# Moving the last 64 rows of a weight onto four DMA engines in a decode kernel: gated attention and MLP on one core

## The chip, the cores and the metric

The kernel runs on one core of a Trainium2 chip. The core has a matrix engine (TensorE; its matmuls are "PE" in the profile and its weight loads "PEld"), a vector engine (DVE), a scalar engine (ACT), a general engine (POOL), a sequencer that here only issues transfers (SP), and 16 DMA engines that carry data from the chip's memory (HBM) into the on-chip memory of 128 partitions (SBUF). The metric is the device time of one execution in microseconds.

## The reference

One decode step for a batch of 8 with a model width of 448. Attention: 16 query heads on 8 key/value heads, each 256 wide, over the last 1024 positions of the cache. Beside it a small MLP (448 to 1792 to 448). A sigmoid gate mixes the two. All tensors are bf16.

```
g = sigmoid((x * gate_w).sum(-1))
q = x @ wq                                   # 448 x 4096
p = softmax(q k^T * 256**-0.5)               # k, v: last 1024 rows of the caches
a = (p v) @ wo                               # 4096 x 448
b = gelu(layernorm(x) @ w1 + b1) @ w2 + b2
out = g * a + (1 - g) * b
```

The K and V that are read make 64 MB, wq and wo 3.5 MB each, w1 and w2 1.5 MB each.

## The kernel before

Everything is loaded once. SP issues nearly all transfers, in one written order: w1 (`w1_sb`, L159; its last 64 rows `w1_t`, L162), w2 (L164), three pieces of wq of 128 rows (`wq_sb`, L167), the last 64 rows of wq (`wq_t`, L168), and then a list of units: 32 K tiles and 32 V tiles of 1 MB (`load`, L148; one tile holds two batches of one head), and eight pieces of wo (`wo_sb`, L187), one behind every fourth K tile and the eighth at the very end. The last V tile comes in two halves. `issue_to` (L182) issues units as long as one of the 12 buffers for K and V is free; its first call, `issue_to(NKV)`, stands at L200, before the small constants are built. Each transfer that SP issues also waits until the transfer eight places earlier has landed, since eight completion counters are used in turn. x, b1, b2 and later gate_w are issued by ACT (L156 to L158, `gate_load`).

The small constants (an identity, ones, masks, zeroed pads) are written by DVE and POOL at L203 to L230. Then x and its normalised form y are turned into columns: `halves` spreads the last 64 entries of a row over even and odd places of two rows of 128, `transposed` turns five pieces with TensorE and copies the result to `xT` and `yT`. The MLP follows (`mlp_up` L311, `mlp_down` L347), then q: for each of 32 blocks of 128 columns of wq, the block is the stationary side and `xT` (8 columns) the moving side, so q comes out with its head dimension on the partitions. 96 matmuls take `wq_sb`, 32 take `wq_t` (L377), which holds each of the 64 rows as two half rows on two partitions. Two scaled copies (L389) write `qT`.

The main loop has 64 steps. A step turns half a K tile with 16 transposes (`transposes`, L407; copies L412), makes the scores of the step before (`scores`, L433), and eleven steps behind them the product with V (`pv`, L508). After four V tiles, `o_scale` (L519) and `o_proj` (L533) multiply a head's output by its piece of wo, into one PSUM bank that all heads share. At the end `o_proj(7)` runs 8 matmuls, DVE applies the gate (L577), and SP and ACT each send half of the result (L581).

Of the kernel before, what the change touches and what calls it, by code (L numbers as in the profile page):

```python
# [16 lines left out]
def kernel(  # L17
# [38 lines left out]
    HH = HD // 2  # L56
    assert Sq == 1 and Dh % P == 0 and W % P == 0 and F % P == 0
    FH = F // 2
    NH = NF // 2
    assert TL * 2 == P and NC * R <= 2 * P and NB % TB == 0 and 3 * 32 <= P and R <= 32 and NF % 2 == 0  # L60
    qscale = float(Dh) ** -0.5
    NU = NBU * Hkv
    NSTEP = NU * TB
# [2 lines left out]
    NKV = 12  # L66
# [4 lines left out]
    CP = 32  # L71
# [37 lines left out]
    wq_t = big.tile([P, HH], BF16, name="wq_t")  # L109
    w1_sb = big.tile([P, DC, F], BF16, name="w1_sb")  # L110
    wo_sb = [big.tile([P, NKH, D], BF16, name=f"wo_sb{g}") for g in range(Hkv)]
# [3 lines left out]
    gw_sb = consts.tile([NB, D], BF16, name="gw_sb")  # L115
# [11 lines left out]
    xT = consts.tile([P, DC + 2, NB], BF16, name="xT")  # L127
    yT = consts.tile([P, DC + 2, NB], BF16, name="yT")
    x_e = consts.tile([NB, 2, P], BF16, name="x_e")
# [11 lines left out]
    def load(kind, n):  # L141
        t = kvpool.tile([P, NC, Dh], BF16, tag="kv", name="kv")
        src = A_k_cache if kind == "K" else A_v_cache
        g, u = divmod(n, NBU)
        parts = TB if (kind, n) == ("V", NU - 1) else 1
        w = NC // parts
        for q in range(parts):
            nc.sync.dma_start(  # L148
                t[:, q * w : (q + 1) * w, :].rearrange("p c d -> p (c d)"),
                src[u * TB : (u + 1) * TB, g, kv0:Sk, :].rearrange(  # L150
                    "t (r c) d -> r t c d", c=NC
                )[:, :, q * w : (q + 1) * w, :].rearrange("r t c d -> r t (c d)"),
            )
        KV[kind, n] = t
# [27 lines left out]
    def issue_to(k):  # L182
        while pos[0] < len(units):
            kind, n = units[pos[0]]
            if kind == "W":
                r0 = n * NKH * P
                nc.sync.dma_start(  # L187
                    wo_sb[n][:].rearrange("p (i j) n -> p i (j n)", i=rep),
                    A_wo[r0 : r0 + NKH * P, :].rearrange(
                        "(i p j) n -> p i (j n)", i=rep, j=NJ  # L190
                    ),
                )
# [39 lines left out]
    prod = consts.tile([NB, D], F32, name="prod")  # L232
# [7 lines left out]
    y_sb = consts.tile([NB, D], BF16, name="y_sb")  # L240
# [27 lines left out]
    def transposed(dst, t, t_e):  # L268
        v = t[:, 0:DM].rearrange("b (p c) -> b c p", c=DC)
        parts = [v[:, c, :] for c in range(DC)] + [t_e[:, h, :] for h in range(2)]  # L270
        tp = ps_kt.tile([P, W], BF16, tag="ktp", name="tp")
        for c, part in enumerate(parts):
            nc.tensor.transpose(
                tp[:, c * NB : (c + 1) * NB], part, ident[0:NB, 0:NB]
            )
        nc.vector.tensor_copy(
            dst[:], tp[:, 0 : len(parts) * NB].rearrange("p (c b) -> p c b", b=NB)
        )

    halves(y_e, y_sb)  # L280
    transposed(yT, y_sb, y_e)
    halves(x_e, x_sb)
    transposed(xT, x_sb, x_e)


    def gate_load():
        src = gate_w.rearrange("(o d) -> o d", o=1)
        nc.scalar.dma_start(gw_sb[:], src.to_broadcast([NB, D]))

    def gate():  # L290
        nc.vector.tensor_tensor(prod[:], x_sb[:], gw_sb[:], op=ALU.mult)
# [13 lines left out]
        nc.vector.tensor_copy(gg4[:], A_bank[0:PT, DN : DN + 2])  # L305
        nc.vector.tensor_scalar_mul(bvec[:], bsum[:], gg4[:, 1:2])
# [58 lines left out]
    mlp_down()  # L365


    q_ps = ps_g.tile([P, 512], F32, tag="grp", name="q_ps")
    NQ = Hq * NJ
    for c in range(DC + 1):  # L370
        for k in range(NQ):
            if c < DC:
                w, xs = wq_sb[:, c, k * P : (k + 1) * P], xT[:, c, :]
            else:
                h, kk = divmod(k, NQ // 2)
                w, xs = wq_t[:, kk * P : (kk + 1) * P], xT[:, DC + h, :]
            nc.tensor.matmul(  # L377
                q_ps[:, k * NB : (k + 1) * NB],
                lhsT=w,
                rhs=xs,  # L380
                start=(c == 0 and k == 0),
                stop=(c == DC),
                skip_group_check=True,
            )
    q_v = q_ps[:, 0 : Hq * NJ * NB].rearrange(
        "p (g i j b) -> p i j g b", i=rep, j=NJ, b=NB
    )
# [158 lines left out]
    for n in range(LAST):  # L546
# [5 lines left out]
        g, r = divmod(n, SPG)  # L552
# [7 lines left out]
        m = n - SPG - LAG  # L560
# [51 lines left out]
```

## Time and profile before

| what | value |
|---|---|
| median of 3 runs | 196.95 us (196.83 to 197.05) |
| the profiled execution, its own time | 196.92 us |
| its span, first to last instruction | 195.2 us |
| busy: PE, PEld, DVE | 164.2, 153.6, 113.1 us |
| busy: ACT, POOL | 6.4, 2.8 us |
| moved | 78.14 MB, mean 400 GB/s |
| last 64 rows of wq | 1 transfer of 512 KB, 14.5 us from issue to landing |
| last piece of wo | 1 transfer of 448 KB, issued at 174.03 us, landed at 191.33 us |

The profile is one execution. It gives busy time by engine, the waits, the chain of work that ended last, and a record of each DMA packet with its queue, size, start and duration, though not the number of the DMA engine that carried it. Queue q1 holds what SP issues, q10 what ACT issues, q8 and q14 instructions that the chip fetches for its own engines. A packet is one run of bytes: a wq or K tile gives packets of 8 KB, `wq_t` of 4 KB, a wo piece of 1792 B. On each engine, a transfer ends with a packet of 4 B, which counts the completion.

### The profile page before, as it was taken

The numbers are of one execution on the slowest core, as the hardware profiler recorded it, in microseconds if no ns is written. First come the engines' busy times: TensorE is split into PE (matmuls) and PEld (weight loads), VectorE is DVE, ScalarE is ACT, GpSimd is POOL, SyncE is SP. The second block draws the span as 40 slices with busy tenths as digits, with TensorE's granted clock in tenths as the row PEclk, the third lists the DMA queues.
The fourth block names the chain that finished last, engine by engine and source line by source line (L and its number), as shares of the span: only waits on it lengthen the run. The fifth ranks groups of instructions, "written<-read, shape, count | busy, mean of one in ns | idle before, by whom it ended". The sixth has DMA issues, their size and how long they took to land.

```text
span 195.2 us, 7355 instructions
## 1 busy us (share of the span) xinstructions
PE 164.2 (84%) x3417; PEld 153.6 (79%) x3417; DVE 113.1 (58%) x255; ACT 6.4 (3%) x13; POOL 2.8 (1%) x16
## 2 busy tenths in 40 slices
PE   2677799988899796958999898988898989989752
PEld 1565799988899796957999797978897989989541
DVE  3122189996477653764559674964586646766401
ACT  5000000000000000010000000000000000000000
POOL 5000000000000000000000000000000000000000
PEclk9999889997569855585569996995599655699555
DMA  6999999999999999999999999999999999999940
GB/s 215 412 426 425 425 413 426 426 423 420 421 426 422 417 425 426 425 417 431 423 423 419 422 425 428 418 421 418 425 430 417 421 425 430 426 420 425 394 176 5
DMA packets 12769, 78.14 MB, mean 400 GB/s; under 512 B 1330, under 2 KB 3523, under 8 KB 4164
## 3 DMA queue, kind: packets, MB, share of 16 engines
q1 hardware_dynamic: 12688, 77.67, 95.4%
q8 instruction: 26, 0.43, 0.8%
q10 hardware_dynamic: 52, 0.02, 0.0%
q14 instruction: 3, 0.02, 0.0%
HBM read 77.68 MB, written 0.01 MB: 398 GB/s over the span
## 4 chain that ended last, share of the span: by engine, by line
DMA 91%; PE 6%; SPq 1%; issue 0%; DVE 0%
DMA kv<-in_A_k_cache_dram 47%; DMA kv<-in_A_v_cache_dram 19%; DMA wo_sb<-in_A_wo_dram 18%; DMA wq_sb<-in_A_wq_dram 7%; PE ktp L407 4%; PE grp L433 1%; PE A_bank L533 0%; PE grp L508 0%; SPq L167 0%; PE grp L422 0%; SPq L164 0%; DVE res L577 0%; SPq L159 0%; SPq L162 0%; SPq L148 0%
## 5 line engine op out<-in xcount | busy, mean ns | idle before, releaser
L412 DVE COPY kt<-ktp 128x1024 bf16<-128x1024 bf16 x128 | 84.4, 687 | 44.4 <-PE ktp L407 43.9
L407 PE MATMUL ktp<-ident,kv 128*128 128x128 bf16 x1024 | 89.0, 257 | 7.9 <-DMA kv<-in_A_k_cache_dram 6.7
L407 PEld LDWEIGHTS <-kv 128*128 128x128 bf16 x1024 | 78.0, 118 | 10.9 <-DMA kv<-in_A_k_cache_dram 7.9
L508 PE MATMUL grp<-e,kv 128*128 128x4 bf16 x1024 | 35.6, 166 | 2.6 <-DMA kv<-in_A_v_cache_dram 2.5
L508 PEld LDWEIGHTS <-kv 128*128 128x128 bf16 x1024 | 32.6, 101 | 5.6 <-DMA kv<-in_A_v_cache_dram 2.8
L433 PE MATMUL grp<-qT,kt 128*128 128x4 bf16 x1024 | 36.6, 166 | 0.3 <-DVE kt L412 0.2
L433 PEld LDWEIGHTS <-kt 128*128 128x128 bf16 x1024 | 34.6, 100 | 1.8 <-issue 0.6
L482 ACT ACTIVATE e<-grp 128x256 bf16<-128x256 f32 x8 | 3.1, 383 | 161.8 <-PE grp L475 161.8
L491 PE MATMUL A_bank<-zs,onesf 128*128 128x16 f32 x16 | 3.6, 299 | 4.5 <-DVE zs L487 4.5
L491 PEld LDWEIGHTS A_bank<-zs,onesf 128*128 128x128 f32 x16 | 2.8, 218 | 5.1 <-DVE zs L487 5.1
L533 PE MATMUL A_bank<-wo_sb,ot 128*8 128x224 bf16 x64 | 5.5, 305 | 0.8 <-DMA wo_sb<-in_A_wo_dram 0.5
L321 PE MATMUL h_ps<-yT,w_sb 128*128 128x8 bf16 x42 | 4.2, 195 | 1.2 <-DMA w_sb<-in_B_w_dram 1.2
L495 DVE RECIPROCAL rz<-A_bank 128x16 f32<-128x16 f32 x8 | 2.1, 258 | 5.4 <-PE A_bank L491 5.4
L519 DVE TENSOR_TENSOR ot<-grp,rz 128x32 bf16<-128x32 f32 x8 | 1.5, 186 | 6.4 <-PE grp L508 6.4
L487 DVE TENSOR_REDUCE zs<-e 128x16 f32<-128x256 bf16 x8 | 4.8, 602 | 0.0
L353 PE MATMUL b_ps<-w_sb,hT 128*8 128x224 bf16 x28 | 2.8, 388 | 2.4 <-DVE b_ps L349 2.4
L338 DVE COPY z<-h_ps 128x112 f32<-128x112 f32 x1 | 0.3, 275 | 7.7 <-PE h_ps L329 7.7
L321 PEld LDWEIGHTS <-w_sb 128*128 128x128 bf16 x42 | 3.6, 152 | 1.3 <-DMA w_sb<-in_B_w_dram 1.3
L475 PE MATMUL grp<-diag,onesb 128*128 128x256 bf16 x8 | 2.5, 308 | 2.2 <-DVE diag L469 1.9
L353 PEld LDWEIGHTS <-hT 128*8 128x8 bf16 x28 | 1.8, 121 | 3.0 <-DVE hT L344 2.2
L446 DVE TENSOR_REDUCE pm<-grp 128x16 f32<-128x256 f32 x8 | 3.3, 415 | 0.6 <-PE grp L433 0.6
L533 PEld LDWEIGHTS <-ot 128*8 128x8 bf16 x64 | 2.6, 93 | 1.3 <-issue 0.4
(82 smaller groups left out, 53.6 us busy)
## 6 DMA issues: line engine op xcount, KB each, us to landing
kv<-in_A_k_cache_dram SPq DMA_DIRECT2D x32, 1024.0 KB, 18.3
kv<-in_A_v_cache_dram SPq DMA_DIRECT2D x31, 1024.0 KB, 18.3
wo_sb<-in_A_wo_dram SPq DMA_DIRECT2D x8, 448.0 KB, 18.3
wq_sb<-in_A_wq_dram SPq DMA_DIRECT2D x3, 1024.0 KB, 12.1
w_sb<-in_B_w_dram SPq DMA_DIRECT2D x1, 1568.0 KB
w_sb<-in_B_w_dram SPq DMA_DIRECT2D x1, 1344.0 KB, 5.9
kv<-in_A_v_cache_dram SPq DMA_DIRECT2D x2, 512.0 KB, 19.8
wq_t<-in_A_wq_dram SPq DMA_DIRECT2D x1, 512.0 KB, 14.5
```

Source lines behind the costliest of these rows:

```text
L321: nc.tensor.matmul(o, lhsT=cols(w1_sb[:, c, h * FH : (h + 1) * FH]), rhs=yT[:, c, :], start=(c == 0), stop=False,)
L353: nc.tensor.matmul(b_ps[CP * j : CP * j + NB, 0:DN], lhsT=M["hT"][:, k * NB : (k + 1) * NB] if k < NF else onesb[0:1, 0:NB], rhs=w2_sb[:, ...
L407: nc.tensor.transpose(ktp[:, c * P : (c + 1) * P], K[:, h * HC + c, j * P : (j + 1) * P], ident[:],)
L412: nc.vector.tensor_copy(kt[:, j, :], ktp[:])
L433: nc.tensor.matmul(G[g][:, s : s + RU], lhsT=kt[:, j, c * P : (c + 1) * P], rhs=qT[:, j, g, bu * TB : (bu + 1) * TB, :].rearrange("p t i - ...
L446: nc.vector.reduce_max(pm[:], G[g][:, S0 : S0 + NC * R].rearrange("p (c r) -> p r c", r=R), axis=AXIS.X,)
L475: nc.tensor.matmul(G[g][:, S0 : S0 + NC * R].rearrange("p (c r) -> p c r", c=NC), lhsT=onesb[:], rhs=diag[g % 2][:].unsqueeze(1).to_broadc ...
L482: nc.scalar.activation(e[:], G[g][:, S0 : S0 + NC * R], ACT.Exp)
L487: nc.vector.reduce_sum(zs[:], E[g][:].rearrange("p (c r) -> p r c", r=R), axis=AXIS.X)
L491: nc.tensor.matmul(zc, lhsT=onesf[:], rhs=zs[:], start=False, stop=True, skip_group_check=True)
L508: nc.tensor.matmul(G[g][:, o : o + RU], lhsT=V[:, cc, :].rearrange("p (q j) -> p j q", j=NJ)[:, j, :], rhs=E[g][:, cc * R + bu * RU : cc * ...
L533: nc.tensor.matmul(A_bank[CP * j : CP * j + NB, 0:DN], lhsT=ot[:].rearrange("p j (b i) -> p j i b", i=rep)[:, h, i, :], rhs=wo_sb[g][:, k, ...
```

## The change

The last 64 rows of wq are stored and loaded in another way, and several things follow from it.

1. `wq_t` is no tile of its own any more. It is a view of the first 48 partitions of a new tile `wo_hi`, which later receives the wo pieces of heads 3 to 7. A partition holds two neighbouring rows of wq, a run of 16 KB; partitions 0 to 15 and 32 to 47 are used. Two transfers bring 16 partitions each, with a source written as 4 by 4 by 8192 elements. POOL first writes zeros over the 48 partitions. These transfers, and with them `issue_to(NKV)`, stand behind the small constants in the program.
2. q is computed with x as the stationary side (`xT` padded to 32 columns) and wq as the moving side, 512 columns at a time. Four matmuls write four strips of 32 partitions of one PSUM tile, for two tiles and five pieces of rows: 40 matmuls in place of 128. Then DVE and ACT each scale one tile into `q_r`, 8 transposes turn it, and four copies write `qT`.
3. `pairs` replaces `halves` for x, `transposed` makes two copies instead of one, and `xT` is zeroed by POOL.
4. The last piece of wo comes in two transfers of 224 KB.
5. `gw_sb` becomes a view of `w1_sb`.

```
-    nc.sync.dma_start(wq_t[:], A_wq[DM:D, :].rearrange("r (h n) -> (r h) n", h=2))
...
+    TQ, TH, TP = 2, 16, 48
+    NHI = 5
+    wo_sb = [big.tile([P, NKH, D], BF16, name=f"wo_sb{g}") for g in range(Hkv - NHI)]
+    wo_hi = big.tile([P, NHI * NKH * D], BF16, name="wo_hi")
+    wq_t = wo_hi[0:TP, 0 : TQ * HD].rearrange("p (q n) -> p q n", q=TQ)
...
+    gw_sb = w1_sb[0:NB, 0, 0:D]
...
-                nc.sync.dma_start(
-                    wo_sb[n][:].rearrange("p (i j) n -> p i (j n)", i=rep),
...
+                dst = wo_sb[n][:, :, :].rearrange("p (i j) n -> p i (j n)", i=rep)
...
+                if n < Hkv - 1:
+                    nc.sync.dma_start(dst, src)
+                else:
+                    for i in range(rep):
+                        nc.sync.dma_start(dst[:, i, :], src[:, i, :])
...
-    issue_to(NKV)
...
+    nc.gpsimd.memset(xT[:], 0.0)
...
+    nc.gpsimd.memset(wq_t, 0.0)
+    for h in range(2):
+        nc.sync.dma_start(
+            wq_t[32 * h : 32 * h + TH].rearrange("p q n -> p (q n)"),
+            A_wq[DM + TL // 2 * h : DM + TL // 2 * (h + 1), :].rearrange(
+                "(r i q) n -> i r (q n)", i=4, q=TQ
+            ),
+        )
+    issue_to(NKV)
...
+    def pairs(dst, src):
+        for h in range(2):
+            nc.vector.tensor_copy(
+                dst[:, :, 32 * h : 32 * h + TH].rearrange("b q (i r) -> b q i r", i=4),
+                src[:, DM + TL // 2 * h : DM + TL // 2 * (h + 1)].rearrange(
+                    "b (r i q) -> b q i r", i=4, q=TQ
+                ),
+            )
...
-    for c in range(DC + 1):
-        for k in range(NQ):
...
-            nc.tensor.matmul(
-                q_ps[:, k * NB : (k + 1) * NB],
-                lhsT=w,
-                rhs=xs,
...
+    for c, (w, xs) in enumerate(wq_c):
+        for t in range(NT):
+            for k in range(NS):
+                n0 = QW * (NS * t + k)
+                nc.tensor.matmul(
+                    q_ps[t][CP * k : CP * (k + 1), :],
+                    lhsT=xs,
+                    rhs=w[:, n0 : n0 + QW],
...
+                    tile_position=(0, CP * k),
...
-    for i in range(rep):
-        nc.vector.tensor_scalar_mul(qT[:, :, :, :, i], q_v[:, i], qscale)
+    nc.vector.tensor_scalar_mul(q_r[:, 0:QW], q_ps[0][:], qscale)
+    nc.scalar.activation(q_r[:, QW : 2 * QW], q_ps[1][:], ACT.Copy, scale=qscale)
+    q_tp = ps_kt.tile([P, W], BF16, tag="ktp", name="q_tp")
+    for t in range(NT):
+        for k in range(rep * NJ):
+            o = (t * rep * NJ + k) * P
+            nc.tensor.transpose(q_tp[:, o : o + P], q_r[:, o : o + P], ident[:])
...
+    for t in range(NT):
+        for i in range(rep):
+            nc.vector.tensor_copy(
+                qT[:, :, NS * t : NS * (t + 1), :, i], q_v[:, t, i, :, :, 0:NB]
+            )
```

More of the change, by code (lines that the diff above doesn't have):

```diff
@@ L55 @@
     TL = D - DM
-    HH = HD // 2
+    TQ, TH, TP = 2, 16, 48
     assert Sq == 1 and Dh % P == 0 and W % P == 0 and F % P == 0
@@ L59 @@
     NH = NF // 2
-    assert TL * 2 == P and NC * R <= 2 * P and NB % TB == 0 and 3 * 32 <= P and R <= 32 and NF % 2 == 0
+    assert TL * 2 == P and TL == 2 * TH * TQ and NC * R <= 2 * P and NB % TB == 0 and 3 * 32 <= P and R <= 32 and NF % 2 == 0
     qscale = float(Dh) ** -0.5
@@ L108 @@
     wq_sb = big.tile([P, DC, HD], BF16, name="wq_sb")
-    wq_t = big.tile([P, HH], BF16, name="wq_t")
     w1_sb = big.tile([P, DC, F], BF16, name="w1_sb")
-    wo_sb = [big.tile([P, NKH, D], BF16, name=f"wo_sb{g}") for g in range(Hkv)]
+    NHI = 5
+    wo_sb = [big.tile([P, NKH, D], BF16, name=f"wo_sb{g}") for g in range(Hkv - NHI)]
+    wo_hi = big.tile([P, NHI * NKH * D], BF16, name="wo_hi")
+    wo_sb += [
+        wo_hi[:, k * NKH * D : (k + 1) * NKH * D].rearrange("p (k n) -> p k n", n=D)
+        for k in range(NHI)
+    ]
+    wq_t = wo_hi[0:TP, 0 : TQ * HD].rearrange("p (q n) -> p q n", q=TQ)
+    assert TQ * HD <= NHI * NKH * D
     w1_t = big.tile([P, FH], BF16, name="w1_t")
@@ L114 @@
     x_sb = consts.tile([NB, D], BF16, name="x_sb")
-    gw_sb = consts.tile([NB, D], BF16, name="gw_sb")
+    gw_sb = w1_sb[0:NB, 0, 0:D]
     b1_sb = consts.tile([1, F], BF16, name="b1_sb")
@@ L126 @@
     qT = consts.tile([P, NJ, Hkv, NB, rep], BF16, name="qT")
-    xT = consts.tile([P, DC + 2, NB], BF16, name="xT")
+    xT = consts.tile([P, DC + TQ, CP], BF16, name="xT")
     yT = consts.tile([P, DC + 2, NB], BF16, name="yT")
-    x_e = consts.tile([NB, 2, P], BF16, name="x_e")
+    x_e = consts.tile([NB, TQ, TP], BF16, name="x_e")
     y_e = consts.tile([NB, 2, P], BF16, name="y_e")
@@ L186, in issue_to @@
                 r0 = n * NKH * P
-                nc.sync.dma_start(
-                    wo_sb[n][:].rearrange("p (i j) n -> p i (j n)", i=rep),
-                    A_wo[r0 : r0 + NKH * P, :].rearrange(
-                        "(i p j) n -> p i (j n)", i=rep, j=NJ
-                    ),
-                )
+                dst = wo_sb[n][:, :, :].rearrange("p (i j) n -> p i (j n)", i=rep)
+                src = A_wo[r0 : r0 + NKH * P, :].rearrange(
+                    "(i p j) n -> p i (j n)", i=rep, j=NJ
+                )
+                if n < Hkv - 1:
[3 more added lines that the diff above has]
+                        nc.sync.dma_start(dst[:, i, :], src[:, i, :])
             else:
@@ L266, in halves, with transposed @@
             )
-    def transposed(dst, t, t_e):
+    def pairs(dst, src):
[6 more added lines that the diff above has]
+            )
+    def transposed(dst, t, t_e, n):
         v = t[:, 0:DM].rearrange("b (p c) -> b c p", c=DC)
@@ L273, in transposed @@
             nc.tensor.transpose(
-                tp[:, c * NB : (c + 1) * NB], part, ident[0:NB, 0:NB]
+                tp[0 : part.shape[-1], c * NB : (c + 1) * NB], part, ident[0:NB, 0:NB]
             )
-        nc.vector.tensor_copy(
-            dst[:], tp[:, 0 : len(parts) * NB].rearrange("p (c b) -> p c b", b=NB)
-        )
+        for lo, hi, m in ((0, DC, P), (DC, DC + 2, n)):
+            nc.vector.tensor_copy(
+                dst[0:m, lo:hi, 0:NB],
+                tp[0:m, lo * NB : hi * NB].rearrange("p (c b) -> p c b", b=NB),
+            )
     halves(y_e, y_sb)
-    transposed(yT, y_sb, y_e)
-    halves(x_e, x_sb)
-    transposed(xT, x_sb, x_e)
+    transposed(yT, y_sb, y_e, P)
+    pairs(x_e, x_sb)
+    transposed(xT, x_sb, x_e, TP)
     def gate_load():
         src = gate_w.rearrange("(o d) -> o d", o=1)
-        nc.scalar.dma_start(gw_sb[:], src.to_broadcast([NB, D]))
+        nc.scalar.dma_start(gw_sb, src.to_broadcast([NB, D]))
     def gate():
-        nc.vector.tensor_tensor(prod[:], x_sb[:], gw_sb[:], op=ALU.mult)
+        nc.vector.tensor_tensor(prod[:], x_sb[:], gw_sb, op=ALU.mult)
         nc.vector.reduce_sum(gsum[:], prod[:], axis=AXIS.X)
@@ L365 @@
     mlp_down()
-    q_ps = ps_g.tile([P, 512], F32, tag="grp", name="q_ps")
-    NQ = Hq * NJ
-    for c in range(DC + 1):
-        for k in range(NQ):
[L372 to L376, printed above, removed]
-            nc.tensor.matmul(
-                q_ps[:, k * NB : (k + 1) * NB],
-                lhsT=w,
-                rhs=xs,
-                start=(c == 0 and k == 0),
-                stop=(c == DC),
-                skip_group_check=True,
-            )
@@ L385 @@
-    q_v = q_ps[:, 0 : Hq * NJ * NB].rearrange(
-        "p (g i j b) -> p i j g b", i=rep, j=NJ, b=NB
-    )
-    for i in range(rep):
-        nc.vector.tensor_scalar_mul(qT[:, :, :, :, i], q_v[:, i], qscale)
+    QW = 512
+    NS = P // CP
+    NT = HD // (NS * QW)
+    assert QW == rep * NJ * P and NT * NS == Hkv
+    q_ps = [ps_g.tile([P, QW], F32, tag="grp", name="q_ps") for _ in range(NT)]
+    wq_c = [(wq_sb[:, c, :], xT[:, c, :]) for c in range(DC)]
+    wq_c += [(wq_t[:, k, :], xT[0:TP, DC + k, :]) for k in range(TQ)]
@@ new lines @@
+    for c, (w, xs) in enumerate(wq_c):
[6 more added lines that the diff above has]
+                    rhs=w[:, n0 : n0 + QW],
+                    start=(c == 0),
+                    stop=(c == len(wq_c) - 1),
+                    tile_position=(0, CP * k),
+                    skip_group_check=True,
+                )
@@ new lines @@
+    q_r = ktpool.tile([P, NJ, W], BF16, tag="kt", name="q_r")
+    q_r = q_r[:].rearrange("p j w -> p (j w)")
+    nc.vector.tensor_scalar_mul(q_r[:, 0:QW], q_ps[0][:], qscale)
[5 more added lines that the diff above has]
+            nc.tensor.transpose(q_tp[:, o : o + P], q_r[:, o : o + P], ident[:])
@@ L392 @@
+    q_v = q_tp[:].rearrange(
+        "p (t i j s z) -> p t i j s z", t=NT, i=rep, j=NJ, s=NS
+    )
+    for t in range(NT):
+        for i in range(rep):
+            nc.vector.tensor_copy(
+                qT[:, :, NS * t : NS * (t + 1), :, i], q_v[:, t, i, :, :, 0:NB]
+            )
     KT = {}
```

## Prediction

> **What bounds the kernel now.** I read the page first: its slices of the span, its queues, its chain.
>
> ```profile
> DMA  6999999999999999999999999999999999999940
> GB/s 215 412 426 425 425 413 426 426 423 420 421 426 422 417 425 426 425 417 431 423 423 419 422 425 428 418 421 418 425 430 417 421 425 430 426 420 425 394 176 5
> ...
> q1 hardware_dynamic: 12688, 77.67, 95.4%
> q8 instruction: 26, 0.43, 0.8%
> ...
> DMA 91%; PE 6%; SPq 1%; issue 0%; DVE 0%
> ```
>
> The DMA engines are full in all slices but the first and the last two (the third last is down to 394 GB/s), and the chain is 91% DMA. So the time is the bytes of the slowest engine. The queue's tail is what matters: asked by stretches, the trace gives for each its length, the busy time of PE, PEld, DVE, ACT and POOL, the PE clock, the DMA share and GB/s.
>
> ```profile
> 175.70:180.60 4.90, 4.66 (x137) 4.43 (x135) 3.06 (x6) 0.00 (x0) 0.00 (x0) 0.92 1.00 425
> 180.60:185.40 4.80, 3.35 (x72) 2.74 (x70) 2.13 (x10) 0.38 (x1) 0.00 (x0) 0.50 0.95 389
> 185.40:190.30 4.90, 2.65 (x83) 2.40 (x84) 0.26 (x1) 0.00 (x0) 0.00 (x0) 0.50 0.45 178
> ```
>
> From 185.4 us less than half of the engines carry anything: they do not end together. Which ones end late comes from the single packets. A packet of one size always takes the same time, and the next of its engine starts 3 ns before it ends, so the packets of q1 can be strung by start and end into 16 strings, each with the same 792 packets. Start to start: 70.5 ns for 1792 B, 155 for 4 KB, 306 for 8 KB, 400 for 10.5 KB, a straight line of 37 ns per KB. The strings end so (us; * carried one of the eight 896 B packets of the eight-row `gate_w` load):
>
> ```
> no PE code packet (8):   184.69* 184.76* 184.80* 185.14 185.15* 185.16* 185.41 186.50*
> three of them (6):       189.35 189.40 189.44 189.44 189.45* 189.61
> four of them (2):        190.24* 190.99
> ```
>
> The 26 code packets of 16 KB (q8; one per 263 PE instructions, 6834 in all) fall on only eight strings, in a fixed round. Each holds its engine up by 1.41 us (16 KB beside an 8 KB packet take 1.717 us, the latter alone 0.306). Three make the 4.2 us between the groups. The 186.50 string has two 8 KB packets of q14.
>
> Then the end, by the timeline:
>
> ```profile
> 190.24 0.58 PE L508 MATMUL grp<-e,kv 128*128 128x4 bf16 x16 [0.64 <-DMA kv<-in_A_v_cache_dram]
> 190.86 0.19 DVE L519 TENSOR_TENSOR ot<-grp,rz 128x32 bf16<-128x32 f32 x1 [5.05 <-PE grp L508]
> 191.37 0.91 PE L533 MATMUL A_bank<-wo_sb,ot 128*8 128x224 bf16 x8 [0.54 <-DMA wo_sb<-in_A_wo_dram]
> 192.32 0.44 DVE L577 SCALAR_TENSOR_TENSOR res<-A_bank,gg,bvec 64x224 bf16<-64x224 f32 x1 [1.26 <-PE A_bank L533]
> ```
>
> The last packet ends at 190.99, its 8 matmuls start 0.38 later, and what follows is fixed.
>
> **The change part by part.** The sum stands against this execution: 196.92 us, 195.2 of them span, 0.03 below the median.
>
> *wq's last rows.* Before, each engine carries 8 packets of 4 KB and a 4 B one: 1.25 us. After, the source's outer dimension is 4. In the trace the engines follow the outer dimension: 128 rows lie on 16 strings, the 8 rows of `gate_w` on 8, the single rows of b1 and b2 both on one of these 8 (184.80). So four rows should lie on four of the eight starred strings. Two of these take code packets, second and third of the round; the six others of the round lie outside the eight. If the round goes through neighbouring engines, these two are the last of the eight, as the first takes none: the four have none. Each then carries 8 packets of 16 KB. No row has that size in q1: 0.608 us by the straight line, 1.41 by the code packet. I take 0.608, the same queue and direction. That is 4.87 less 1.25, +3.63 us: from 184.69 to 185.16 they move to 188.3 to 188.8, and the 186.50 string, if among them (three places for five strings, 3 in 5), to 190.13. The twelve others lose 1.25: 188.4 at most with three code packets, 189.74 with four. PE has 160 instructions less, so the 26th code packet (186.6 us, 190.24 string) comes when the queue is done; the 25th still comes in time. The last packet ends at 190.13 (3 in 5) or 189.74: −0.86 or −1.25.
>
> [...]
>
> *wo's last piece.* Only 4 of the 8 matmuls need the second half. On the slowest engine the last V half ends 1.14 us before wo; `pv` to `ot` take 0.39 + 0.58 + 0.19 + 0.05, so the first four can start 0.2 after the last packet and not 0.38: −0.17. Bounds 0 and −0.46 (half of 0.91).
>
> *SP and POOL.* POOL's zeros: start to start 0.045 us for 16 elements (`diag`), 0.14 for 128, 0.24 for 256: 0.8 ns an element, 8192 take 6.6, from 3.5 to 10.2 us. SP holds `wq_t` (6.70 before) until then, and behind it the first K (7.07 before, about 11.1 after), three more K's and the first wo. The first string is done with `wq_sb` at 17.16, a transfer's first packet comes 1.04 after its issue (w1: 0.80, 1.84), so the cover is 5 us; with zeros at twice the price 12 engines run dry for 0.6 us. The extra transfer moves each later wait one landing on: the fifth K waits for `wq_sb` (18.4) instead of 15.95, with 10.9 us of K and wo still queued. Nothing.
>
> *q.* Before, 128 matmuls, 2.60 + 0.96 us. Now 40 of 512 columns: L353 and L533 start their two strips 7 ns apart and pairs 92 or 187 ns apart for 224 columns, so four strips of 512 take 0.21 to 0.43, ten groups 2.1 to 4.3 (8.5 if strips did not overlap). The last four groups wait for `wq_t`: strings end `wq_sb` at 17.2 to 18.0, plus 4.87, plus 0.35: 22.4 to 23.3, where 21.26 was. Then 0.9 to 1.7 of matmuls, 0.6 to 0.7 to scale (ACT 0.38 for 256 columns, DVE 0.28 for 112), 0.8 to 1.2 of transposes (16 in 1.05 to 1.89), four copies of about 0.2 (`yT` 0.18) beside the first K transposes. K work starts at 25.0 to 26.9 and not 23.54; K itself lands 24.9 to 25.5. PE is 1.5 to 3.4 late, and the first V's and K's on those four engines too. Queue and cover: a transfer takes 18.3 us from issue to landing, so SP's issue may slip by over 10 us before an engine runs dry. PE waits 9.2 us for K and V in all, 7.9 after the first; it must gain 3.4 + 1.0 by the end. Hidden; without that cover up to +3.
>
> *The rest.* DVE's extra copies (0.18 each, before w1 lands at 6.7), `xT` zeros (0.14), `gw_sb` in `w1_sb`, whose readers ended 50 us earlier: nothing.
>
> Sum: 196.92 − 0.86 − 0.17 = 195.9 us, or 195.5 if the 186.50 string is not among the four.
>
> **Rivals.**
> Slower, code engines: the four include one with code packets. 189.45 + 3.63 = 193.08, that is 198.8 us (199.6 with the 190.24 string). It decides once one of the four is a string past 187.4. For it: two of the eight are such; against it: their place in the round. 7%. [...]
> Slower, dear packets: a 16 KB packet takes more than 0.72 us with the 186.50 string (0.88 without) and eats the gain; at the code packet's own 0.95 it is 198.6, at 1.41 over 201. Against it the straight line up to 10.5 KB. 7%.
> Slower, PE: it does not catch up and the tail waits for it, up to 197 to 199. Against it eight waits of PE for K spread to 159 us. 5%.
> The split by four does not happen: each engine carries two 16 KB packets (1.22 us) and only the wo halves count: 196.75, within the 0.2% that a measurement of this kernel can tell from no change. 8%.
>
> **How the numbers follow.** The forecast has 73%: 195.9, with a range of its own of 195.2 (189.74 and a full −0.46) to 196.2. Low is 195.0, for the fourth code packet coming late as well. High is 197.0: the no-split case and small losses of the PE and packet cases are inside, the code engines and dear packets are left out. Faster 74%, same 9%, slower 17%.
>
> **What would show it.** Right: q1 with 16 KB packets and as many bytes; the share in the last stretches fuller and shorter; `wq_t` landing about 3 us later than before and K work from 25 to 27 us; the last wo landing near 190.2 to 190.5; 4 matmuls of L533's successor after it; 25 code packets inside the queue. Wrong: a last landing past 191.3, DMA shares under 1 near 18 us (SP late), or no PE wait for V after 180 us.

## The result, and the profile after

| what | before | after |
|---|---|---|
| median, side by side | 196.95 us (196.83 to 197.05, 5 executions) | 196.09 us (195.99 to 196.31, 5 executions) |
| the profiled execution, its own time | 196.92 us | 196.05 us |
| its span | 195.2 us | 194.0 us |
| busy: PE, DVE, POOL | 164.2, 113.1, 2.8 us | 159.4, 119.8, 9.7 us |

The ratio is 0.9958, with a 95% interval of 0.9944 to 0.9973: faster by 0.4%. The forecast was 195.9 us with a range of 195.0 to 197.0. In a second series of twelve executions the changed kernel had eight between 195.96 and 196.36, and four at 197.4 to 198.5; these four are the subject of the last experiments.

From the page of the kernel after: the slices, two queues, and the shares of the chain.

```profile
GB/s 210 413 432 432 424 416 427 422 418 419 425 429 422 417 422 426 427 414 431 422 422 425 418 424 421 432 414 426 419 426 418 424 429 421 426 421 427 409 253 8
...
q1 hardware_dynamic: 12600, 77.67, 96.0%
q8 instruction: 26, 0.43, 0.8%
...
DMA 46%; PE 39%; DVE 11%; issue 1%; ACT 0%; DVEq 0%; SPq 0%
```

The bytes of q1 are the same (77.67 MB). The last two full slices went from 394 and 176 to 409 and 253 GB/s: the end is fuller and shorter. The chain now goes much more through PE and DVE. That is new and will matter, though the transfers still end last. The three stretches of the end, with the same columns as before (length, busy time of PE, PEld, DVE, ACT and POOL, PE clock, DMA share, GB/s):

```profile
175.70:180.60 4.90, 4.02 (x122) 3.68 (x120) 3.36 (x10) 0.00 (x0) 0.00 (x0) 1.00 1.00 419
180.60:185.40 4.80, 4.16 (x99) 3.59 (x98) 1.71 (x7) 0.38 (x1) 0.00 (x0) 0.64 0.93 384
185.40:190.30 4.90, 2.27 (x68) 1.94 (x65) 0.19 (x1) 0.00 (x0) 0.00 (x0) 0.50 0.49 193
```

The single packets, strung into 16 strings as before the change, end so (us; * carried a `gate_w` packet):

```
no PE code packet, no 16 KB packets (4):      183.62* 183.81 183.98 184.37*
eight 16 KB packets of wq, no code (4):       188.42* 188.58* 188.67* 190.22* (two q14 packets)
three code packets (7):                       187.97 to 188.23, two of them starred (188.12* 188.21*)
four code packets (1):                        189.48
```

The 4 B packets that count completions went from 1288 to 1296 in q1. The old `wq_t` transfer had 16, the second half of wo adds 16, so the two new transfers have 8 together: four engines each. The last packet is at 190.22 where it was at 190.99. The end by the timeline:

```profile
189.45 0.58 PE L558 MATMUL grp<-e,kv 128*128 128x4 bf16 x16 [0.65 <-DMA kv<-in_A_v_cache_dram]
190.07 0.19 DVE L569 TENSOR_TENSOR ot<-grp,rz 128x32 bf16<-128x32 f32 x1 [5.17 <-PE grp L558]
190.32 0.91 PE L583 MATMUL A_bank<-wo_hi,ot 128*8 128x224 bf16 x8 [0.28 <-DVE ot L569]
191.27 0.44 DVE L627 SCALAR_TENSOR_TENSOR res<-A_bank,gg,bvec 64x224 bf16<-64x224 f32 x1 [1.01 <-PE A_bank L583]
```

L558 is the old L508, L583 the old L533, L627 the old L577. The eight matmuls of L583 wait for `ot` now, not for wo; the gate multiplication starts at 191.27 where it started at 192.32: 1.05 us earlier, of which 0.77 are the last packet and 0.28 the closer distance behind it (0.10 and not 0.38 us from the last packet to L583).

Of these 1.05 us the measured time shows 0.87 (196.92 to 196.05). The span is shorter by 1.2, since from the gate multiplication to its end it takes 2.7 us where it took 2.9; but the time outside the span, the execution's own time less its span, went from 1.72 to 2.05 us. The profile does not show what lies there.

### The profile page after: what moved, and what is told of

It reads as the page before. It is cut to its first block, busy times and chain, and to the rows that moved or that the text cites. A ratio compares the mean times of both kernels' runs of the same rounds, so it can differ in the third digit from the quotient of the medians.

```text
span 194.0 us, 7209 instructions
## 1 busy us (share of the span) xinstructions
PE 159.4 (82%) x3337; PEld 146.9 (76%) x3337; DVE 119.8 (62%) x260; ACT 7.0 (4%) x14; POOL 9.7 (5%) x18
## 3 DMA queue, kind: packets, MB, share of 16 engines
q1 hardware_dynamic: 12600, 77.67, 96.0%
## 4 chain that ended last, share of the span: by engine, by line
DMA 46%; PE 39%; DVE 11%; issue 1%; ACT 0%; DVEq 0%; SPq 0%
DMA kv<-in_A_k_cache_dram 27%; PE ktp L457 20%; DMA kv<-in_A_v_cache_dram 18%; PE grp L483 6%; PE grp L558 4%; DVE y_sb L269 3%; DVE kt L462 3%; PE A_bank L583 2%; PE b_ps L387 2%; PE q_ps L413 1%; PE h_ps L355 1%; PE h_ps L363 1%; PE h_ps L359 1%; DMA x_sb<-in_A_x_dram 1%; DVE zs L537 1%
## 5 line engine op out<-in xcount | busy, mean ns | idle before, releaser
L457 PE MATMUL ktp<-ident,kv 128*128 128x128 bf16 x1024 | 84.3, 249 | 5.9 <-DMA kv<-in_A_k_cache_dram 5.9
L457 PEld LDWEIGHTS <-kv 128*128 128x128 bf16 x1024 | 73.8, 114 | 8.9 <-DMA kv<-in_A_k_cache_dram 6.8
L558 PE MATMUL grp<-e,kv 128*128 128x4 bf16 x1024 | 35.6, 165 | 3.6 <-DMA kv<-in_A_v_cache_dram 2.7
L558 PEld LDWEIGHTS <-kv 128*128 128x128 bf16 x1024 | 32.4, 100 | 5.6 <-DMA kv<-in_A_v_cache_dram 3.0
L483 PEld LDWEIGHTS <-kt 128*128 128x128 bf16 x1024 | 34.1, 100 | 1.7 <-DVE kt L462 0.5
L244 POOL MEMSET wo_hi<- 48x8192 bf16 x1 | 6.9, 6914 | 0.0
L269 DVE TENSOR_SCALAR y_sb<-x_sb,mv,rstd 8x448 bf16<-8x448 bf16 x1 | 6.5, 6505 | 0.0
L583 PE MATMUL A_bank<-wo_hi,ot 128*8 128x224 bf16 x40 | 3.8, 332 | 0.3 <-DVE ot L569 0.3
```

The costliest lines, as they stand in the source:

```text
L244: nc.gpsimd.memset(wq_t, 0.0)
L269: nc.vector.tensor_scalar(y_sb[:], x_sb[:], scalar1=mv[:, 0:1], scalar2=rstd[:], op0=ALU.subtract, op1=ALU.mult,)
L457: nc.tensor.transpose(ktp[:, c * P : (c + 1) * P], K[:, h * HC + c, j * P : (j + 1) * P], ident[:],)
L483: nc.tensor.matmul(G[g][:, s : s + RU], lhsT=kt[:, j, c * P : (c + 1) * P], rhs=qT[:, j, g, bu * TB : (bu + 1) * TB, :].rearrange("p t i - ...
L558: nc.tensor.matmul(G[g][:, o : o + RU], lhsT=V[:, cc, :].rearrange("p (q j) -> p j q", j=NJ)[:, j, :], rhs=E[g][:, cc * R + bu * RU : cc * ...
L583: nc.tensor.matmul(A_bank[CP * j : CP * j + NB, 0:DN], lhsT=ot[:].rearrange("p j (b i) -> p j i b", i=rep)[:, h, i, :], rhs=wo_sb[g][:, k, ...
```

## The experiments

All run against the kernel before on the same chip, which gave medians of 196.69 to 196.80 us there. A ratio below is to that, with its 95% interval.

### The changed kernel again

No edit.

> The changed kernel again, beside the others on one chip. 196.1 us, span 194.0 to 194.2; the last packet of the last wo piece ends near 190.2 us on the string that carries 16 KB packets and two q14 packets, the string with four code packets near 189.5.

Measured: median 196.22 (0.9996, 0.9968 to 1.0023): eight executions of 195.96 to 196.36, and 197.41, 197.67, 198.41, 198.48. The kernel before had none above 197.2 in its 23 of the same chip. The gain of the usual execution repeats; the long ones are new, and an interval that holds them no longer excludes "no change".

### The same rows over all sixteen engines

```
-                "(r i q) n -> i r (q n)", i=4, q=TQ
+                "(r i q) n -> i r (q n)", i=16, q=TQ
...
-                dst[:, :, 32 * h : 32 * h + TH].rearrange("b q (i r) -> b q i r", i=4),
+                dst[:, :, 32 * h : 32 * h + TH].rearrange("b q (i r) -> b q i r", i=16),
...
-                    "b (r i q) -> b q i r", i=4, q=TQ
+                    "b (r i q) -> b q i r", i=16, q=TQ
```

> Outer dimension 16 in place of 4 for the last rows of wq; runs of 16 KB, q in rows and wo's halves stay. Theory (the gain is the bytes that the code-packet engines no longer carry): each engine has two 16 KB packets, 1.22 us; the string with four code packets ends at 189.48 + 1.22 = 190.70, and the end moves by 0.48 us: 196.6 us. Rival (long runs, q in rows and later issue make the gain): as the changed kernel, 196.1.

Measured: 200.53 us (1.0187, 1.0173 to 1.0202), 4 us above what was expected. The 16 KB packets, 0.611 us each in the changed kernel, took 0.61 to 2.41 us here, 2.15 in the median. The page's row of rates, by slice of 5 us:

```profile
GB/s 209 414 430 326 181 425 419 425 420 419 424 424 429 417 425 420 425 424 425 420 429 424 412 429 420 424 422 427 422 424 419 424 425 422 422 429 424 416 202 7
```

In the fourth and fifth slice, where `wq_t` is written, the rate falls to 326 and 181 GB/s (432 and 424 in the changed kernel). In the changed kernel four strings carry these rows, eight 16 KB packets each. By the layout sixteen engines carry them here, each with one partition of each half, so four engines write in every group of four neighbouring partitions, where in the changed kernel one does; the dearest packets take 3.9 times 0.611 us. The price of a 16 KB packet is not fixed; the next three runs change the layout.

### Six engines on partitions in one block

The rows on partitions 0 to 31, 30 of them by a transfer of outer dimension 6, two by one of 2; no zeros are needed.

```
-    TQ, TH, TP = 2, 16, 48
+    TQ, TH, TP = 2, 16, 32
...
+        wq_t[0:30].rearrange("p q n -> p (q n)"),
+        A_wq[DM : DM + 60, :].rearrange("(r i q) n -> i r (q n)", i=6, q=TQ),
+    )
+    nc.sync.dma_start(
+        wq_t[30:32].rearrange("p q n -> p (q n)"),
+        A_wq[DM + 60 : D, :].rearrange("(i q) n -> i (q n)", q=TQ),
```

> The last rows of wq over six engines (30 runs of 16 KB with outer dimension 6, two more with outer dimension 2) on partitions 0 to 31, no zeros by POOL. Theory: the string with q14 packets has five or six 16 KB packets and not eight and ends at 188.4 to 189.0; the string with four code packets is the last, 189.48: minus 0.74 us, 195.4. If a fifth or sixth engine carries code packets it is 188.2 + 3.0 = 191.2 and 197.0. Rival (the engines do not matter): 196.1. Rival (partitions out of step with the engines slow the packets down): 16 KB packets over 0.61 us each.

Measured: 200.74 us (1.0206, 1.0184 to 1.0228). Again slow packets: seven of the 32 take 0.91 to 2.26 us, the others 0.611, and 66 of the 8 KB packets that start in the first 25 us take longer than their 0.309 us (none in the changed kernel); one slice falls to 273:

```profile
GB/s 214 415 428 427 273 420 431 426 418 412 427 430 422 412 430 428 422 419 429 422 425 419 417 432 422 417 419 426 425 422 416 424 430 423 425 420 428 366 106 7
```

So packets are dear here with six engines of five partitions each (0 to 4, 5 to 9 and on), far fewer than sixteen. By the layout (the profile does not name the engines) no partition is written by two engines within one of these transfers. What the layouts of the two slow kernels have in common is that several engines write in one group of four partitions (0 to 3, 4 to 7 and on): four in every group with sixteen engines, two or more in five of the eight groups here.

### Six engines in step

Rows of 8 KB, 24 on partitions 0 to 23 and 24 on 32 to 55 with outer dimension 6, sixteen on 0 to 15 with outer dimension 4. By the layout every group of four partitions then belongs, within these transfers, to one engine, as it does in the changed kernel (0 to 3 and 32 to 35 to the first, and on); "in step" stands for this.

```
+    WQT = ((0, 0, 0, 6, 24), (32, 24, 0, 6, 24), (0, 48, 1, 4, 16))
...
+    for k in range(4):
+        nc.gpsimd.memset(wq_t[0:32, 0, k * 1024 : (k + 1) * 1024], 0.0)
+    for p0, r0, q, i, m in WQT:
+        ...
+            wq_t[p0 : p0 + m, q, :],
+            A_wq[DM + r0 : DM + r0 + m, :].rearrange("(r i) n -> i r n", i=i),
```

> The last rows of wq as runs of 8 KB in three transfers: 24 rows with outer dimension 6 on partitions 0 to 23, 24 rows likewise on 32 to 55, 16 rows with outer dimension 4 on 0 to 15; zeros of half the width in four pieces. [...] Theory: no packet is slowed (8 KB packets stay at 0.309 us); engines 0 to 3 carry 3.7 us of it, 4 and 5 2.4; the q14 string ends at 185.35 + 3.67 = 189.0, the four-code-packet string is last at 189.5: minus 0.74 us against the changed kernel, 195.4, none above 197. Rival (only the number of engines counts, not the partitions): the same. Rival (engines 4 or 5 carry code packets): 188.2 + 2.4 = 190.6, 196.5.

Measured: no packet is slowed (8 KB packets take 0.309 us in the changed kernel), so it was not the number six. What differs is the layout, and the size of the packets (8 KB here; the next run has 16 KB ones). Still 196.38 us (0.9994, 0.9976 to 1.0012), 196.15 at best, 197.65 and 198.0 at worst, where 195.4 and none above 197 was expected: the last packet is at 190.19, on a starred string that carries three code packets and its share of wq. One of the two engines that were added fetches code. The two starred strings without any wq packet end at 183.47 (no code) and 187.67 (three). So one code engine is among the fifth and sixth of the eight, one among the seventh and eighth; the first four have none.

### Eight engines, one transfer, no zeros

```
-    TQ, TH, TP = 2, 16, 48
+    TQ, TH, TP = 2, 16, 32
...
-    nc.gpsimd.memset(wq_t, 0.0)
...
+        wq_t.rearrange("p q n -> p (q n)"),
+        A_wq[DM:D, :].rearrange("(r i q) n -> i r (q n)", i=8, q=TQ),
```

> One transfer with outer dimension 8, four runs of 16 KB for each of the first eight engines, on partitions 0 to 31, no zeros. Theory: partitions are in step with the engines, so 16 KB packets take 0.61 us again, not 1 to 2.4 as with outer dimensions 16 and 6; two of the eight carry code packets and end at 188.2 + 2.43 = 190.6: plus 0.4 us, 196.5, none above 197. Rival (any transfer that is not on the four engines collides): packets over 0.61 us and 199 to 201 us.

Measured: all 16 KB packets take 0.611 us (by the layout four neighbouring partitions to each engine, in step). Median 196.18 (0.9979, 0.9958 to 0.9999): five executions at 195.77 to 195.89, four at 196.13 to 196.57, three at 197.2 to 197.7. In the profiled one (195.79) the last packet is at 190.20, on a code string with three code packets and four of the 16 KB ones; the span is 194.1 (194.0 in the changed kernel), so its 0.26 us of advantage lie outside the span (1.69 and not 2.05). `y_sb` is back at 0.38 us and K work starts at 23.22. The long executions stay with the early K start. That would clear the late K start of the changed kernel of blame, but they may have a cause of their own in this kernel: the last experiment shows one.

### The last wo piece whole, and the halves alone

The changed kernel with `if True:` for `if n < Hkv - 1:` in `issue_to`:

> The changed kernel with wo's last piece in one transfer. Theory: the last packet stays at 190.2 and the first matmul of the last head waits for it, 0.38 after and not 0.10 as now: plus 0.28 us, 196.4. Rival (the halves are most of the gain): near 196.9.

Measured: median 196.49 (0.9999, 0.9982 to 1.0016), eight executions of 196.29 to 196.54 and four of 197.0 to 198.3; the usual one is 0.3 us longer than in the changed kernel. Its end by the timeline:

```profile
190.24 0.19 DVE L569 TENSOR_TENSOR ot<-grp,rz 128x32 bf16<-128x32 f32 x1 [4.11 <-PE grp L558]
190.48 0.08 PEld L583 LDWEIGHTS <-ot 128*8 128x8 bf16 x1 [0.37 <-DVE ot L569]
190.73 0.91 PE L583 MATMUL A_bank<-wo_hi,ot 128*8 128x224 bf16 x8 [0.53 <-DMA wo_hi<-in_A_wo_dram]
```

`ot` is ready at 190.43, and the matmuls wait for wo's landing till 190.73. With halves they wait for `ot` alone. The same edit alone, in the kernel before:

> The kernel before with only the last wo piece in two transfers. Theory: the slowest engine still ends at 190.99, the first matmul of the last head starts when its input is ready (191.1) and not at 191.37: minus 0.27 us, 196.6. Rival (halves move nothing by themselves): 196.85.

Measured: 196.53 us (0.9986, 0.9977 to 0.9994), 0.26 us below the kernel before, and no execution above 196.71. The halves are worth 0.26 to 0.3 us either way.

### q in rows alone, and the old q in the changed kernel

The first adds to the kernel before the halves and the whole q part of the change (40 matmuls, the two scaled copies, 8 transposes, 4 copies), with the old `wq_t`.

> The kernel before with wo's halves and q in rows on four strips; wq's last rows still in one transfer on all engines, in the old place. Theory (q is hidden, the bytes per engine decide): as with the halves alone, 196.5 us. If q in rows, or what it does to TensorE's start, makes the executions of 197.4 and more that the changed kernel, e2, e6 and e7 showed, some of these lie above 197.2; if those come from transfers that end earlier on 12 engines, none.

Measured: 196.51 us (0.9988, 0.9980 to 0.9997), none above 197.0: the halves alone gave 196.53, so q in rows gives nothing here. This kernel differs from the changed one only in wq's last rows and what serves them (the zeros, the later issue, the two views). It is 0.24 us faster than the kernel before beside it, and the usual executions of the changed kernel 0.75 to 0.86: by that difference wq's rows are worth 0.5 to 0.6 us. The second puts the blocks of 128 columns back behind the new load:

```
+    for c in range(DC + TQ):
+        for k in range(NQ):
+            if c < DC:
+                w, xs = wq_sb[:, c, k * P : (k + 1) * P], xT[:, c, 0:NB]
+            else:
+                w = wq_t[:, c - DC, k * P : (k + 1) * P]
+                xs = xT[0:TP, c, 0:NB]
```

> The changed kernel with q computed as before (blocks of wq as the stationary side, 160 matmuls; the last rows in two pieces of 48 partitions), four engines, zeros and wo's halves kept. Theory: the last packet stays at 190.2, 196.1 us, or 196.3 as the 26th code packet is 224 instructions earlier. If the four engines make the long executions, about one in three lies above 197.2; if q in rows makes them, none.

Measured: 195.86 us (0.9963, 0.9946 to 0.9979), the best median of all: ten executions of 195.56 to 196.00, and 197.07 and 197.28. The spans of the ten are 193.8 to 194.2, as in the changed kernel, so their advantage too lies outside the span. And with two long ones here and none in the run before, q in rows is not what makes the long executions. The profile caught the 197.07 one. The last packet is where it should be, at 190.24. But:

```profile
185.55 0.37 PE L509 MATMUL grp<-diag,onesb 128*128 128x256 bf16 x1 [1.35 <-DVE diag L503]
185.72 1.30 PE L542 MATMUL grp<-e,kv 128*128 128x4 bf16 x32
186.95 0.91 PE L567 MATMUL A_bank<-wo_hi,ot 128*8 128x224 bf16 x8
187.79 0.59 PE L542 MATMUL grp<-e,kv 128*128 128x4 bf16 x16
188.25 0.59 PE L525 MATMUL A_bank<-zs,onesf 128*128 128x16 f32 x2
188.67 2.70 PE L542 MATMUL grp<-e,kv 128*128 128x4 bf16 x96
191.66 0.91 PE L567 MATMUL A_bank<-wo_hi,ot 128*8 128x224 bf16 x8 [0.28 <-DVE ot L553]
```

From 185.7 on no line here waits for a transfer. 96 V matmuls stand in one row without a gap, behind them L567 at 191.66, 1.34 us later than in the changed kernel (190.32). In this execution TensorE had not caught up when the data ended, and it set the end. It fell behind only near the end: at 160.01 us it still waited 1.20 us for a K tile.

```profile
160.01 1.12 PE L441 MATMUL ktp<-ident,kv 128*128 128x128 bf16 x16 [1.20 <-DMA kv<-in_A_k_cache_dram]
```

From 160 to 175 us its granted clock was 0.53 and from there to 192 it was 0.60, where the profiled execution of the changed kernel had 0.77 and 0.70, that of the kernel before 0.68 and 0.64. So in this execution the late K start had been made up long before, and the lower clock of the last 30 us is the likely cause; one such execution was profiled.

### Zeros in eight pieces

```
-    nc.gpsimd.memset(wq_t, 0.0)
+    for q in range(TQ):
+        for k in range(4):
+            nc.gpsimd.memset(wq_t[:, q, k * 1024 : (k + 1) * 1024], 0.0)
```

> The changed kernel with POOL's zeros in eight pieces of 1024 columns. Theory: DVE's y_sb no longer waits for the whole 6.9 us; it takes at most 1.3 us, the MLP starts 4 us earlier and K work starts near 24 to 25.5 us and not at 27.8. The last packet stays at 190.2, so the usual time is the same, 196.1; but if the executions of 197.4 to 198.5 that the changed kernel showed are TensorE not catching up, there are none above 197. Rival (those long executions come from the transfers): they stay, about one in three.

This was to let DVE's `y_sb` end between the pieces. Two lines of the kernel after show what it was meant to mend, a POOL and a DVE instruction with busy time and mean duration (ns):

```profile
L244 POOL MEMSET wo_hi<- 48x8192 bf16 x1 | 6.9, 6914 | 0.0
L269 DVE TENSOR_SCALAR y_sb<-x_sb,mv,rstd 8x448 bf16<-8x448 bf16 x1 | 6.5, 6505 | 0.0
```

The DVE one took 0.38 us in the kernel before. It starts at 3.99, inside POOL's instruction (3.45 to 10.36), and ends at 10.49, 0.13 behind it. With eight pieces of POOL (from 3.46, 7.2 us in all) it becomes, by the groups of the tile `y_sb` (least, median and largest duration in ns, start):

```profile
L271 DVE TENSOR_SCALAR y_sb<-x_sb,mv,rstd x1: 5970/5970/5970, 4.8 to 4.8; 8x448 bf16<-8x448 bf16 x1
```

It still ends only behind the last piece, at 10.78, and K work starts at 27.64 (27.78). So the edit did not do what it was for, and as a test of what the late K start costs it is void. 196.09 us (0.9965, 0.9953 to 0.9977), the same as the changed kernel.

### Half of the score matmuls left out

```
-        for c in range(HC):
+        for c in range(HC // 2):
             for j in range(NJ):
                 s = S0 + (h * HC + c) * R + bu * RU
```

> The changed kernel with half of the score matmuls left out (8 of the 16 of every step), so the output is not the reference's. It moves the same bytes in the same order; TensorE has 512 matmuls less, and with them about four code packets less. Theory (the executions of 197 to 198.5 us are those in which TensorE has not caught up when the data ends): the usual execution stays at 196.0 to 196.3, since its last packet at 190.2 is on a string without code packets, and none of twelve executions lies above 197.0. Rival (they come from the transfers, the four full strings above all): two to four of twelve stay above 197.0. If the usual time itself falls below 195.7, TensorE was also setting the end of the usual execution.

Measured: 196.06 us (0.9968, 0.9956 to 0.9980), five executions within 196.03 and 196.14; 22 code packets and not 26; last packet 190.30. The usual execution does not move, so TensorE does not set its end. No execution is long. That agrees with the theory but does not settle it: if 4 of 17 are long in the changed kernel, five out of five are usual in about one series of four.

### Eight engines with the old q

This joins the transfer of outer dimension eight and the old blocks of q.

> The one transfer of outer dimension eight onto partitions 0 to 31 (no zeros by POOL), together with the halves of wo and with q computed as before in blocks (160 matmuls). From the two runs that it joins: the transfer of eight with q in rows had its usual executions at 195.8 to 195.9, the old blocks in the changed kernel 195.6 to 196.0 against 196.0 to 196.3 with rows. If the two gains add, the usual execution is 195.5 to 195.7; if both only bring the time down to what the last packet (190.2) allows, 195.6 to 195.9. Executions above 197.0: some, as in both, if TensorE's lateness makes them.

Measured: 197.0 us (1.0012, 0.9987 to 1.0036), six of twelve executions at 197.45 to 198.38 and six at 195.91 to 196.54. The gains do not add. The profile is of a long execution (197.45), and it is not TensorE this time:

```profile
189.88 0.59 PE L535 MATMUL grp<-e,kv 128*128 128x4 bf16 x16 [0.78 <-DMA kv<-in_A_v_cache_dram]
191.10 0.58 PE L535 MATMUL grp<-e,kv 128*128 128x4 bf16 x16 [0.64 <-DMA kv<-in_A_v_cache_dram]
191.97 0.91 PE L560 MATMUL A_bank<-wo_hi,ot 128*8 128x224 bf16 x8 [0.28 <-DVE ot L546]
```

TensorE waits for the last V until 191.10. The last packet is at 191.75, on a code engine among the eight that carry wq: code packets at 25.1, 76.6, 131.7 and 186.8. With 112 matmuls more (160 for q, and not 40 and 8 transposes) the 26th code packet came at 186.85, inside the queue, where with q in rows it came at 188.25. There it fell on an engine that was done. A code packet held an engine up by 1.41 us in the kernel before, and 190.2 plus 1.4 to 1.6 is this end. This is the prediction's rival of the code engines, in another kernel. The long executions of the run with q in rows (197.2 to 197.7) lie where the same step would put them, but none of them was profiled.

## Why the prediction was right, point by point

*What bounds it: right.* The time is the slowest engine's bytes. In the usual executions that were profiled, of the changed kernel, with eight engines and with half of the scores, the gate multiplication starts 1.05 to 1.10 us behind the last packet.

*wq's last rows: right, with both of its unsure parts.* The transfers lie on four engines (the 4 B packets), on four starred strings without code packets, and a 16 KB packet takes 0.607 us from start to start where 0.608 was taken from the straight line. The 186.50 string, the one with the two 8 KB packets of q14, was among the four (3 in 5): 190.22, forecast 190.13. The gain of the last packet is 0.77, forecast 0.86. That an outer dimension of four takes the first four of the eight, and that the round goes on to the neighbouring engine, was the author's estimate: the profile names no engine. Counted in the order in which outer dimensions of four, six and eight take them, the reason given for the four being free was only half right: the two starred code engines are not the last two of the eight but one of the fifth and sixth, one of the seventh and eighth. That still leaves the first four free, so the result came out right by some luck. A fifth engine would already have been a risk.

*Dear packets: did not come here, but the rival was real.* In the changed kernel each of the 16 KB packets takes 0.611 us. With the same bytes and sizes on sixteen engines, or on six out of step, they take up to 2.41 and 2.26 and the time is 200.5 to 200.7, near what the rival gave. The prediction looked for the price in the size of a packet. The runs put it in the layout: the split by four onto partitions 0 to 15 and 32 to 47 keeps every engine on groups of four partitions of its own, and so do the splits by six and by eight in step, and these three show no slowed packet (16 KB ones take 0.611 us). The two others do, and all transfers together fall there to 181 GB/s (sixteen engines) and 273 GB/s (six) in the worst slice. Why, and whether it is the number four that counts, no run shows.

*The halves of wo: mechanism right, size off.* −0.17 was forecast (bounds 0 and −0.46), 0.28 measured in the trace and 0.26 to 0.3 by the two runs. The path by `ot` is shorter than it was reckoned: the matmuls start 0.10 us behind the last packet, not 0.2, and all eight run through, so the second half costs nothing.

*POOL's zeros: price right, a side effect missed.* 6.6 us were forecast, 6.91 measured, and `wq_t` was issued at 10.39 (forecast 10.2); no engine ran dry (a DMA share of 0.98 to 1.05 in each 2 us from 10 to 24 us). What was missed is that DVE's `y_sb` ends only behind POOL's zeros: 6.50 and not 0.38 us, so the MLP starts at 11.83 and not 6.73.

```profile
11.83 0.32 PE L355 MATMUL h_ps<-yT,w_sb 128*128 128x8 bf16 x3
...
23.70 2.06 PE L413 MATMUL q_ps<-wq_sb,xT 128*32 128x512 bf16 x24
25.69 1.04 PE L413 MATMUL q_ps<-wo_hi,xT 48*32 48x512 bf16 x16
27.32 0.62 PE L431 MATMUL q_tp<-ident,q_r 128*128 128x128 bf16 x8 [0.59 <-DVE q_r L425]
27.78 1.39 PE L457 MATMUL ktp<-ident,kv 128*128 128x128 bf16 x22
```

*q: the parts right, the sum mis-sized.* The ten groups of four strips take 2.06 and 1.04 us (forecast 2.1 to 4.3), the scaling 0.69 on DVE (0.6 to 0.7), the transposes 0.62 (0.8 to 1.2, too dear). But K work starts at 27.78, forecast 25.0 to 26.9. The prediction had q wait for the last piece of wq, whose packets end at 22.5 (forecast 22.4 to 23.3); it waited for the MLP, which was 5 us late because `y_sb` ended only at 10.49, behind POOL's zeros. The K work was 4.2 us late and not 1.5 to 3.4. In the usual execution the cover held: TensorE is busy without a pause from 30 to 40 us, at 60.19 us it waits for a K tile again, and the second series has eight of twelve executions within 0.5 us of the forecast. That K starts at 23.22 in the run with eight engines and brings no shorter span says the same.

*TensorE not catching up: right in the usual execution, wrong in some.* It was given 5% as a case of its own. It is neither always nor never: 4 of the changed kernel's 17 executions lie at 197.4 to 198.5, in the span of this rival (197 to 199). For the kernel with the old q the profile shows TensorE as the cause. For the changed kernel it is argued, not shown. The granted clock of each execution, the mean over its span, points the same way: 0.771 to 0.791 in the four long ones and 0.782 to 0.824 in the thirteen others, and with the last wo piece whole 0.773 to 0.790 in the four long ones and 0.795 to 0.824 in the eight others. With eight engines it does not divide them (0.756 to 0.808 and 0.753 to 0.805). But none of the changed kernel's long executions was profiled. A late code packet does not explain them: in the profiled execution the twenty-sixth, at 188.3, lies on an engine that had ended by 188.23, and even inside the queue it would end at 189.6 there, below 190.22. The prediction took 7.9 us of waits as TensorE's reserve in one execution, and didn't ask how this varies from one to the next, nor that waits early in the loop are no reserve for the end: the long execution with the old q had still waited at 160 us.

*Outside the span: missed.* The sum left the 1.7 us outside the span as they are. They are 1.96 to 2.06 in the changed kernel and most of its variants, 1.67 to 1.76 in the kernel before, with the halves, with q in rows alone, with the old q, and with eight engines. No single part of the change divides the kernels so. What does is two together: all with the longer time have q in rows and wq's last rows in two or three transfers, and with only one of the two it is the shorter. Why, no run shows. In the path that the prediction reckoned, the last packet came out 0.09 worse and the halves 0.11 better, 1.05 in place of 1.03; 196.92 less 1.05 is 195.87. The 0.18 from there to 196.05 is the 0.33 outside the span less the shorter end of the span, and no term of the sum stood for it.

## What to carry to other kernels

When the transfers bound a kernel, string the packets into engines and look at where each ends: bytes can be moved from the late engines to the early ones with the outer dimension of a transfer (here the last packet came 0.77 us earlier), but only as far as the string with the most code packets and bytes still ends in time, and here the packets kept their price only in layouts that give each engine groups of four neighbouring partitions of its own (0.611 us for 16 KB, up to 2.41 in the two other layouts). Splitting the last transfer, so that each part of the work behind it waits for its own part, was worth its 0.3 us alone here. And moving the end of the transfers forward takes from the reserve of the next engine: measure many executions, not five, since a kernel near two bounds can have two times (here 195.96 to 196.36 us and 197.41 to 198.48).

## What the runs showed of the hardware that was not expected

- A DVE instruction that takes 0.38 us in the kernel before, and in the run with eight engines and no zeros, took 6.50 us beside a POOL memset of 6.91 us and ended 0.13 us behind it. With the same zeros in eight memsets (7.2 us) it took nearly as long (5.97 us). Why, no run shows.
- A 16 KB packet of q1 takes 0.611 us, each of them in eight profiles, where by the layout each engine has groups of four partitions of its own. It takes up to 2.41 us with sixteen engines on 32 partitions, and up to 2.26 with six engines of five partitions each, where 66 packets of 8 KB take longer than their 0.309 us as well.
- The code packets fall on eight of the sixteen strings, two of them among the eight of `gate_w`. Where the 26th of them falls in the last 5 us can decide 1.4 us of time on an engine that also carries more data, as the profiled execution of eight engines with the old q shows (186.85 us, and the last packet at 191.75).
- The 0.3 us outside the span stay open: no run here shows what is done in them.
